# A new order for the compute queues of a linear-attention and gated-MLP kernel, and an earlier release of its weight loads

## The chip, the cores and the metric

The program runs on one core of one Trainium2 chip. The metric is the time of one execution on the device in microseconds (us). The kernel before took 202.53 us in the median of three runs (202.29 to 202.89). One execution was also taken with the hardware profiler; all rows of the profile in this document belong to that one execution.

The engines are named as the profile names them: PE (matmuls), PEld (its weight loads), DVE (vector engine), ACT (scalar engine), POOL (GpSimd) and SP (the queue that issues most DMAs).

## The reference

A block with 2048 rows of width 448: layer norm, an attention whose feature map is a pair of softmaxes, a projection and a residual; then layer norm, a gated MLP with 1792 hidden units, and a residual.

```python
def _A_ref(x, wqkv, w_phi, wo):            # B, S, D = 1, 2048, 448; H, Dh = 16, 28
    qkv = (x @ wqkv).reshape(B, S, 3, H, Dh).transpose(2, 0, 3, 1, 4)
    q, k, v = qkv[0], qkv[1], qkv[2]
    pq = jnp.einsum("bhsd,hdf->bhsf", q, w_phi)
    pk = jnp.einsum("bhsd,hdf->bhsf", k, w_phi)
    phi_q = jnp.concatenate([_softmax(pq), _softmax(-pq)], axis=-1)
    phi_k = jnp.concatenate([_softmax(pk), _softmax(-pk)], axis=-1)
    kv = jnp.einsum("bhsf,bhsd->bhfd", phi_k, v)
    z  = jnp.einsum("bhsf->bhf", phi_k)
    num = jnp.einsum("bhqf,bhfd->bhqd", phi_q, kv)
    den = jnp.einsum("bhqf,bhf->bhq", phi_q, z)[..., None] + 1e-6
    return (num / den).transpose(0, 2, 1, 3).reshape(B, S, D) @ wo

def _B_ref(x, w_gate, w_up, w_down):
    return (_sigmoid(x @ w_gate) * (x @ w_up)) @ w_down

h = x + _A_ref(_layernorm(x), A_wqkv, A_w_phi, A_wo)
h2 = h + _B_ref(_layernorm(h), B_w_gate, B_w_up, B_w_down)
```

## The kernel before

The 2048 rows are cut into 16 tiles of 128 rows. The text uses the names that the code gives to its operations; a trailing number is the tile, or the hidden unit's block of 128 after an underscore.

*First stage (to about 44 us), keys and values.* For each tile `x` is loaded, its statistics are taken on DVE (`bst`, `agg`, L545 and L546), the inverse deviation on POOL (`pow1`, L554) with a negated mean (`nm1`), and it is normalized (`xn`, L573 on DVE, L576 on POOL) into one of three buffers. It is transposed: the first four tiles by PE (`xT0` to `xT3`, L538) with a copy back by DVE or ACT (`xT0e` and so on, L531), the others by DMA from the SP queue. PE multiplies each tile by the folded key weight and by the value weight (`ppa`, `ppb` and `vva`, `vvb` for the first four tiles, then `pva`, `pvb`). Each such product is a pair: its "a" half fills the two row halves of the PE array with two PSUM banks, its "b" half fills them the other way around, so "b" waits until "a" has finished unless other PE work lies between. ACT takes two exponentials of the keys (`ek`, L671 and L672) and copies the values (`v1`, L531). DVE sums (`ss`, L675) and inverts (`rs`, L681), and DVE or POOL makes the normalized features (`phi`, L685) in one of three buffers. PE then adds the features times the values of a tile into two banks that live through the whole stage (`kva`, `kvb`). The query products (`pqa`, `pqb`) and their exponentials on ACT (`eq`, L721) lie between.

*Second stage (about 44 to 59 us), attention.* The finished sums are masked (`kvzA` to `kvzD`), PE forms the sums of the query features (`qs`) and the numerators (`num`), DVE turns these into quotients (`rsm`, `qq`, `b`, `c`, `rden`, L798 to L806), DVE or POOL writes the result (`o`, L810), which is transposed (`oT`) and multiplied by the output weight (`woa`, `wob`). The second normalization follows (`bs2`, `ag2`, `pow2`, `hn`, for later tiles `h`, `sq`, `ve`, `nm`), and a transposition (`hT`).

*Third stage (from about 59 us), the MLP.* PE computes gate and up products for two or four tiles at a time (`ga`, `gb`), ACT takes a tanh (`sig`, L925), DVE multiplies (`hh`, L926) and frees the PSUM banks; then PE does the down products (`dn`, `dp`, at the end `dm`), DVE adds the residual (`fin`, L961) and SP stores. Up to about 105 us the numerators of the remaining tiles and their output projections are interleaved.

*What sets the order.* Every engine executes its operations in the order that a table, `ORDER`, writes out by name, one string for each engine. Which of two engines executes an operation is also read from it: the operation runs on the engine whose string holds its name. Waits follow from the data: an operation waits for what it reads and for the readers of the buffer that it overwrites (`Graph.needs_wait`, `Graph.emit`). Between two operations on DVE, ACT or POOL a wait is added where the second reads the first's result. Two names on PE, `wwo` and `wgu`, do no work: they only wait for the loads of the output weight and of the gate and up weights, so that the first operation behind them takes these waits. `PACE` adds one more dependence: the load `ld_wg1` on the SP queue, and so all loads queued behind it (the rest of the gate, up and down weights), is held until a named PE operation is done.

Of the kernel before, what the change touches and what calls it, by code (L numbers as in the profile page):

```python
# [18 lines left out]
class Graph:  # L19
# [90 lines left out]
    def emit(self, nc):  # L110
# [153 lines left out]
    ),  # L264
    "dve": (
# [21 lines left out]
    ),  # L287
}
PACE = {"ld_wg1": "kva14"}
PROGRAM = (  # L290
# [35 lines left out]
def build(nc, A_x, A_wqkv, A_w_phi, A_wo, B_w_gate, B_w_up, B_w_down, out):  # L326
# [10 lines left out]
    with ExitStack() as es:  # L337
# [658 lines left out]
        at = {o.name: o.i for o in g.ops}  # L996
        for a, b in PACE.items():
            g.ops[at[a]].deps[at[b]] = False
# [36 lines left out]
```

## Time and profile before

| | us |
|---|---|
| median of three runs | 202.53 (202.29 to 202.89) |
| the profiled execution, whole | 202.7 |
| the profiled execution, span from its first to its last instruction | 200.8 |
| PE busy in the span | 195.5 |
| DVE busy in the span | 132.0 |
| ACT busy in the span | 89.4 |
| POOL busy in the span | 56.2 |
| granted TensorE clock, mean | 1.000 |

The span begins with the first instruction and ends with the last; 1.9 us of the execution lie around it. "Busy" counts overlapping instructions of an engine once. Matmuls are pipelined and their ends are modelled, so that a PE shown busy can still be held up for a tenth of a microsecond; the starts of its instructions tell more. Two views are used most below: the chain of waits, which goes back from the last instruction and says at each step what released it, and the timeline, which lists instructions of one engine in order of their start.

### The profile page before, as it was taken

Reading aid. Unit: us, or ns where it says so; the run is one execution under the profiler, and the core shown is the slowest. Engines: PE = TensorE matmul, PEld = TensorE weight load, DVE = VectorE, ACT = ScalarE, POOL = GpSimd, SP = SyncE. Lnnn points to the kernel's source line nnn. Section 1 sums busy time; section 2 is a strip of 40 time slices with the busy share of each in tenths; the row PEclk is TensorE's granted clock in tenths of the full one; section 3 lists DMA queues with packets and bytes.
Section 4 is the critical chain, followed back from the end, with each engine's and each line's share of the span. In section 5 each row is a group of like instructions: output and inputs, shape, how many; then the busy total and the mean of one; then the engine's idle time right before and its main releaser. Section 6 shows DMA issues by size and latency. Waiting matters only on the chain.

```text
span 200.8 us, 5854 instructions
## 1 busy us (share of the span) xinstructions
PE 195.5 (97%) x2516; PEld 114.4 (57%) x2516; DVE 132.0 (66%) x308; ACT 89.4 (45%) x174; POOL 56.2 (28%) x95
## 2 busy tenths in 40 slices
PE   7999999999999999999999999999999999999995
PEld 4835556565568778787444444555555555554443
DVE  5999999978888986576569877346332422272224
ACT  2668988898883451434232432324323212222220
POOL 5779948633343207510170110001400000000000
PEclk9999999999999999999999999999999999999999
DMA  6965346749984230360015220020312000004002
GB/s 157 316 140 129 54 83 76 221 144 302 309 206 66 52 57 15 66 82 3 0 29 124 56 42 10 20 58 26 65 38 52 0 3 2 0 3 137 0 3 91
DMA packets 32490, 16.26 MB, mean 81 GB/s; under 512 B 24720, under 2 KB 31568, under 8 KB 32464
## 3 DMA queue, kind: packets, MB, share of 16 engines
q1 hardware_dynamic: 32336, 15.86, 33.7%
q8 instruction: 20, 0.33, 0.7%
q14 instruction: 6, 0.05, 0.1%
q10 hardware_dynamic: 128, 0.03, 0.1%
HBM read 8.34 MB, written 1.84 MB: 51 GB/s over the span
## 4 chain that ended last, share of the span: by engine, by line
PE 92%; ACT 3%; DMA 2%; issue 1%; SPq 1%; DVE 0%
PE psum L309 84%; PE psum L954 5%; DMA wk_sb<-in_A_wqkv_dram 2%; ACT hhT L671 1%; ACT eq L721 1%; ACT hhT L672 1%; PE psum L524 1%; PE psum L538 1%; PE psum L612 1%; SPq L413 1%; PE psum L599 0%; ACT xnT L531 0%; ACT v L531 0%; DVE x_sb L961 0%
## 5 line engine op out<-in xcount | busy, mean ns | idle before, releaser
L309 PE MATMUL psum<-xnT,wu_sb 64*128 64x512 bf16 (+1 forms) x490 | 93.6, 333 | 0.0
L309 PE MATMUL psum<-xnT,wg_sb 64*128 64x512 bf16 (+1 forms) x490 | 93.5, 333 | 0.1
L925 ACT ACTIVATE sg_sb<-psum 128x512 bf16<-128x512 f32 x56 | 33.2, 596 | 90.1 <-PE psum L309 89.5
L926 DVE SCALAR_TENSOR_TENSOR hhT<-sg_sb,psum 128x512 bf16<-128x512 bf16 x56 | 37.7, 684 | 52.1 <-ACT sg_sb L925 51.7
L309 PEld LDWEIGHTS psum<-xnT,wg_sb 64*128 64x128 bf16 x490 | 44.6, 94 | 20.9 <-DVE hhT L926 2.5
L309 PEld LDWEIGHTS psum<-xnT,wu_sb 64*128 64x128 bf16 x490 | 44.7, 94 | 13.9
L309 PE MATMUL psum<-wd_sb,hhT 64*128 64x448 bf16 x336 | 37.3, 349 | 0.0
L309 PEld LDWEIGHTS psum<-wd_sb,hhT 64*128 64x128 bf16 x336 | 17.8, 94 | 14.2 <-DVE x_sb L836 0.5
L309 PE MATMUL psum<-Wk,xnT 64*128 64x448 bf16 x112 | 22.2, 350 | 0.5 <-ACT hhT L672 0.2
L309 PE MATMUL psum<-wv_sb,xnT 64*128 64x448 bf16 x112 | 22.3, 351 | 0.1
L810 POOL TENSOR_TENSOR o_pad<-c_sb,rden 128x448 bf16<-128x448 bf16 x11 | 10.2, 935 | 28.5 <-DVE rden L806 28.4
L675 DVE TENSOR_REDUCE ss<-hhT 128x32 f32<-128x896 bf16 x16 | 16.8, 1060 | 0.2 <-ACT hhT L672 0.2
L721 ACT ACTIVATE eq<-psum 120x1024 bf16<-120x1024 f32 x16 | 15.6, 1030 | 0.6 <-PE psum L309 0.4
L685 POOL TENSOR_TENSOR phi<-hhT,rs 128x896 bf16<-128x896 bf16 x8 | 13.6, 1710 | 5.6 <-DVE rs L681 3.4
L309 PE MATMUL psum<-xnT,Wq 64*120 64x512 bf16 x112 | 14.8, 383 | 0.3 <-ACT eq L721 0.2
L845 POOL TENSOR_SCALAR ve<-ssq 128x1 f32<-128x1 f32 x11 | 2.2, 201 | 41.8 <-ACT junk L842 41.5
L309 PE MATMUL psum<-wo_o,oT 64*128 64x448 bf16 x56 | 13.2, 350 | 0.0
L309 PE MATMUL psum<-wo_e,oT 64*128 64x448 bf16 x56 | 13.2, 349 | 0.0
L961 DVE SCALAR_TENSOR_TENSOR x_sb<-psum,x_sb 128x448 bf16<-128x448 f32 (+2 forms) x17 | 9.4, 592 | 2.9 <-PE psum L954 1.6
L954 PE MATMUL psum<-wd_sb,hhT 128*128 128x448 bf16 (+2 forms) x70 | 11.2, 316 | 0.0
L309 PEld LDWEIGHTS psum<-Wk,xnT 64*128 64x128 bf16 x112 | 7.8, 94 | 5.8 <-PE psum L309 1.0
L671 ACT ACTIVATE hhT<-psum 128x448 bf16<-128x448 f32 x16 | 8.8, 553 | 4.4 <-PE psum L309 4.2
(105 smaller groups left out, 234.4 us busy)
## 6 DMA issues: line engine op xcount, KB each, us to landing
out_dram<-x_sb SPq DMA_DIRECT2D x15, 112.0 KB, 1.8
x_sb<-in_A_x_dram SPq DMA_DIRECT2D x7, 224.0 KB, 4.2
wd_sb<-in_B_w_down_dram SPq DMA_DIRECT2D x7, 224.0 KB, 5.1
wg_sb<-in_B_w_gate_dram SPq DMA_DIRECT2D x3, 448.0 KB, 5.8
wu_sb<-in_B_w_up_dram SPq DMA_DIRECT2D x3, 448.0 KB, 5.7
wv_sb<-in_A_wqkv_dram SPq DMA_DIRECT2D x2, 224.0 KB, 4.7
wk_sb<-in_A_wqkv_dram SPq DMA_DIRECT2D x2, 196.0 KB, 4.1
wo_e<-in_A_wo_dram SPq DMA_DIRECT2D x1, 336.0 KB, 3.3
```

Of the source, the lines that this page charges most:

```text
L309: p = e.matmul(o, lhsT=w, rhs=r, start=st, stop=sp, tile_position=(row, 0))
L413: return op(eng, name, lambda e: e.dma_start(dst, src), r=r, w=w, dma="in" if eng == "sp" else "ain", nring=48 if eng == "sp" else 8, kb=kb)
L671: e.activation(ek[:, s, :, 0, :], src, ACT.Exp)
L675: op("dve", "ss%d" % t, lambda e: e.tensor_reduce(ss[:, s, :].rearrange("p (b h) -> p b h", h=2), eks.rearrange("p b (d h) -> p b h d", h= ...
L685: return e.tensor_tensor(phi[:, sp, :, :, :].rearrange("p b a n -> p (b a) n")[:, :, 0:56].rearrange("p b (d h) -> p b d h", h=2), eks.rea ...
L721: op("act", "eq%d_%d%s" % (c, i, "pm"[sg]), lambda e, sg=sg: e.activation(eq[c][:, sg, 2 * i:2 * i + 2, :].rearrange("p g n -> p (g n)"), ...
L810: return e.tensor_tensor(o_pad[:, t % NO, off:off + D].rearrange("p (h d) -> p h d", h=H), c_sb[:, t % NS, :, 0:DH], rden[:, t % NS, :][:, ...
L845: op(("pool", "dve"), "ve%d" % t, lambda e: e.tensor_scalar(ve2[:, t:t + 1], ssq2[:, t:t + 1], 1.0 / D ** 3, EPS, op0=ALU.mult, op1=ALU.ad ...
L925: op("act", "sig" + nm, lambda e: e.activation(sg_sb[:, k, 0:W], bk(bg)[:, 0:W], ACT.Tanh, scale=0.5), r=[B(bg)], w=[("sg", k)])
L926: op("dve", "hh" + nm, lambda e: e.scalar_tensor_tensor(out=dst, in0=sg_sb[:, k, 0:W].rearrange("p (f n) -> p f n", n=N), scalar=1.0, in1= ...
L954: p = e.matmul(bk(b)[:, lo:hi], lhsT=hb[:, ff, TS(t)], rhs=wd_sb[:, ff, lo:hi], start=ff == 0, stop=ff == FT - 1)
L961: op("dve", "fin%d%s" % (t, nm), lambda e: e.scalar_tensor_tensor(out=h_sb[:, t, lo:hi], in0=bk(b)[:, lo:hi], scalar=0.5, in1=h_sb[:, t, l ...
```

## The change

Two tables are changed and nothing else: no operation is added or taken away, every operation computes what it did, and the SP queue keeps its order.

`PACE` releases the load `ld_wg1` after `kva12` in place of `kva14`.

In `ORDER` the strings of ACT, PE, DVE and POOL are written anew. Some operations move to another engine: `v1_13` and `oT1e` from DVE to ACT; `kvzD` from DVE to ACT and `kvzA` the other way; `phi10` and `o1` from POOL to DVE and `phi5` from DVE to POOL; `nm1_8` from ACT to POOL; and, from the second normalization, `ve2`, `ve7`, `nm5`, `hn6`, `hn7` and `o10` from POOL to DVE and `ve3`, `ve6`, `nm2`, `nm3` from DVE to POOL. `wwo` moves from between `kva14` and `kvb14` to behind `dn0_11`, behind the first output product `woa0`; `wgu` moves forward to behind `gb0_5`.

```diff
     "act": (
-        "wphi wTe0 wTe2 wTe3 w2e0_0 w2e0_1 w2e0_2 par ek0 xT3e ek1 v1_0 v1_1 nm1_6 ek2 ek3 v1_2 w2e1_1 v1_3 nm1_8 "
...
+        "wphi wTe0 wTe2 wTe3 w2e0_0 w2e0_1 w2e0_2 par xT3e ek0 ek1 v1_0 v1_1 nm1_6 ek3 ek2 v1_2 w2e1_0 v1_3 w2e1_1 "
...
-PACE = {"ld_wg1": "kva14"}
+PACE = {"ld_wg1": "kva12"}
```

Three places show how instructions move. The first is ACT at about 11 us, at the head of the first stage. `COPY xnT` is the copy of tile 3's transpose, `xT3e`; each pair of rows L671 and L672 is one `ek`, for tiles 0 and 1.

```order
 L531 CAST Wk<-psum 128x8x2x28 x3
 L455 CAST par<-mask 128x2
+L531 COPY xnT<-psum 128x4x128
 L671 ACTIVATE hhT<-psum 128x8x56
 L672 ACTIVATE hhT<-psum 128x8x56
-L531 COPY xnT<-psum 128x4x128
 L671 ACTIVATE hhT<-psum 128x8x56
 L672 ACTIVATE hhT<-psum 128x8x56
```

The copy stood between the two `ek` and now stands ahead of both. On PE the transpose `xT3` that feeds it moves in the same way, from behind `ppb0` to between `ppa0` and `ppb0`.

The second place is POOL at about 23 to 28 us. Its rows L685 are `phi4`, the added `phi5`, and `phi7`; L554 is `pow1_12`, and the rows L576 are `xn13` and `xn15`.

```order
 L685 TENSOR_TENSOR phi<-hhT,rs 128x16x56
 L554 TENSOR_TENSOR rst<-mv,neghalf 128x4
+L685 TENSOR_TENSOR phi<-hhT,rs 128x16x56
 L576 TENSOR_SCALAR xn_pad<-x_sb,nm,rst 128x512
 L685 TENSOR_TENSOR phi<-hhT,rs 128x16x56
 L576 TENSOR_SCALAR xn_pad<-x_sb,nm,rst 128x512
```

`phi5` has come to POOL, directly behind `pow1_12`. On DVE, at the same time, these rows stand in the kernel after: `ss5`, `phi3`, `xn11`, `rs5`, `xn12`, `ss6` with `ss7`, `rs6`.

```order
L675 TENSOR_REDUCE ss<-hhT 128x32
L685 TENSOR_TENSOR phi<-hhT,rs 128x16x56
L573 TENSOR_SCALAR xn_pad<-x_sb,mv,rst 128x512
L681 RECIPROCAL rs<-ss 128x32
L573 TENSOR_SCALAR xn_pad<-x_sb,mv,rst 128x512
L675 TENSOR_REDUCE ss<-hhT 128x32 x2
L681 RECIPROCAL rs<-ss 128x32
```

`xn12` (the second row L573) stood behind `ss6` before and now stands right behind `rs5`. `xn12` reads what `pow1_12` writes, and `phi5` stands behind `pow1_12` on POOL, so both come free at nearly the same moment.

The third place is DVE in the MLP stage at about 74 to 78 us. Before, from `rsm9` to `o8`:

```order
L798 RECIPROCAL rsm<-psum 128x16
L799 TENSOR_TENSOR qq<-rsm,psum 128x16
L845 TENSOR_SCALAR ve<-ssq 128x1
L926 SCALAR_TENSOR_TENSOR hhT<-sg_sb,psum 128x2x256
L801 TENSOR_TENSOR b_sb<-psum,qq 128x464
L804 TENSOR_TENSOR c_sb<-b_sb,psum 128x464
L810 TENSOR_TENSOR o_pad<-c_sb,rden 128x448
```

And in the kernel after, again from `rsm9` to `o8`:

```order
L798 RECIPROCAL rsm<-psum 128x16
L799 TENSOR_TENSOR qq<-rsm,psum 128x16
L845 TENSOR_SCALAR ve<-ssq 128x1
L926 SCALAR_TENSOR_TENSOR hhT<-sg_sb,psum 128x2x256
L806 RECIPROCAL rden<-c_sb 128x16
L845 TENSOR_SCALAR ve<-ssq 128x1
L840 TENSOR_SCALAR nm<-sum 128x1
L801 TENSOR_TENSOR b_sb<-psum,qq 128x464
L804 TENSOR_TENSOR c_sb<-b_sb,psum 128x464
L840 TENSOR_SCALAR nm<-sum 128x1
L926 SCALAR_TENSOR_TENSOR hhT<-sg_sb,psum 128x2x256
L810 TENSOR_TENSOR o_pad<-c_sb,rden 128x448
```

The row L926 of the piece before is `hh0_12`; the two of the piece after are `hh0_10` and `hh0_12`. `hh0_12` stood ahead of `b9` and `c9` (L801, L804) and now stands behind them.

82 rows, old and new, of the table ORDER are left out of this document.

## The prediction

> **What bounds the kernel now.** I read the head of the page first, then DVE's forty slices of 5 us and the busy times by stage, then the chain of waits.
>
> ```profile
> span 200.8 us, 5854 instructions
> PE 195.5 (97%) x2516; PEld 114.4 (57%) x2516; DVE 132.0 (66%) x308; ACT 89.4 (45%) x174; POOL 56.2 (28%) x95
> DVE  5999999978888986576569877346332422272224
> PE 92%; ACT 3%; DMA 2%; issue 1%; SPq 1%; DVE 0%
> ```
>
> PE is busy for 195.5 of 200.8 us and holds 92% of the chain of waits. No PE work is removed, so the change can win only what PE waits. The stages show where another engine is full as well (start and end of the stretch, its length, then busy time of PE, PEld, DVE, ACT and POOL, clock, DMA share, GB/s):
>
> ```profile
> 18.00:44.00 26.00, 25.82 (x458) 15.60 (x458) 24.99 (x48) 23.16 (x51) 17.72 (x15) 1.00 0.52 116
> 44.00:59.00 15.00, 14.44 (x255) 8.41 (x249) 12.65 (x37) 13.27 (x19) 5.74 (x7) 1.00 0.97 256
> ```
>
> From 18 to 44 us DVE is busy for 24.99 of 26.00 us: what PE gains at the start counts only if DVE keeps up to tile 15. The places where the chain leaves PE (start, length, what):
>
> ```profile
> 11.34 0.54 ACT hhT L671
> 11.88 0.43 ACT hhT L672
> 12.32 0.48 ACT xnT L531
> 12.79 0.45 ACT hhT L671
> 13.24 0.45 ACT hhT L672
> 13.69 0.14 issue
> 13.82 0.95 PE psum L309 x8
> ...
> 17.45 0.43 ACT v L531
> ...
> 18.02 2.49 PE psum L309 x30
> ...
> 43.55 0.14 issue
> 43.69 0.43 PE psum L309 x16
> 44.12 0.05 issue
> ...
> 47.20 1.95 ACT eq L721 x2
> ...
> 49.19 1.07 PE psum L309 x8
> ```
>
> `ppa2` at 13.82 waits for ACT's `ek0`, `xT3e`, `ek1`; `pva4` at 18.02 waits for the next link of the same ACT queue; `pqa2_1` at 49.19 waits for two `eq`.
>
> **The start.** `xT3e` now runs before `ek0`, while ACT is idle waiting for `ppb0`. Its 0.48 us leave the chain, and `ek1` ends at about 13.2. PE must then be ready earlier too. It is: `xT3` now fills the wait between the halves of `ppa0`/`ppb0`, and `seed` that of `vva0`/`vvb0`. `xT2` slips about 0.2 on DVE behind `agg4`, `agg5`, yet `vva0` starts about 0.1 earlier; `vvb0` ends its issue near 13.37, so `ppa2` starts there: 0.45 earlier. `ppb2`, `ek2`, `v1_2` and `pva4` follow by the same 0.45. Lower bound 0, if `xT2` slips further; upper bound the 0.48 of the row. I take **-0.45**.
>
> **The middle of the first stage.** A lone `kva` between two halves leaves a hole:
>
> ```profile
> 42.22 0.39 PE L309 MATMUL psum<-v,phi 64*128 64x58 bf16 x16
> 42.45 0.86 PE L309 MATMUL psum<-xnT,Wq 64*120 64x512 bf16 x6
> ```
>
> Two kv products issue in 42.45 - 42.22 = 0.23, one in 0.115. `kvb2` moved into the hole behind `pva8` saves **-0.1**; `kvb7` saves nothing, since `pva13` waits there for ACT's `v1_11` anyway. The waits of `wwo` stood between `kva14` and `kvb14`: 0.14 of issue there against 0.05 between `kva15` and `kvb15`, **-0.08**; `woa0` takes them over while it waits for `oT1e`, so they cost nothing there, and 0.1 if that cover is gone. Together -0.63 by `kvb15`.
>
> Can DVE follow? Its last products and the work it hands over:
>
> ```profile
> 42.22 1.14 DVE L685 TENSOR_TENSOR phi<-hhT,rs 128x896 bf16<-128x896 bf16 x2
> L685 DVE TENSOR_TENSOR phi<-hhT,rs 128x896 bf16<-128x896 bf16 x8 | 4.6, 591 | 0.0
> L531 DVE CAST v<-psum 128x448 bf16<-128x448 f32 x1 | 0.6, 617 | 0.0
> ```
>
> It loses `phi5` (0.59) and `v1_13` (0.62) and gains `phi10` (0.59), net 0.6 less, but `xn14` comes early enough to wait about 0.3 for POOL's `xn13`. I put `phi15`'s end at 42.9 against 43.36 now; `kva15` (now 0.115 behind the kv product at 43.69, so 43.8) may then start about 0.14 after that, at 43.05, and PE wants it at 43.2. The 0.14 is the step from the chain above, 13.69 to 13.82. So DVE just keeps up. If it kept its present 43.36, `kva15` could start at 43.5 and 0.3 of the gain would stay. I cap the sum at **-0.55**.
>
> **The loads** leave two kv products earlier, about 2 us. They start now at 43.6 and have all landed before the MLP needs them at 59; no transposition is in flight at 41. Zero, from 0 to -0.1 (`oT2` would find a shorter DMA backlog, but the output product that needs it is not waiting).
>
> **The second stage.** `pqb1_1` moves ahead of `num1`: its `eq` starts 0.23 earlier (two kv-size products issue in that time) and `pqa2_1` with it. It is given back, for `o1` is now DVE work:
>
> ```profile
> 48.47 1.83 POOL L810 TENSOR_TENSOR o_pad<-c_sb,rden 128x448 bf16<-128x448 bf16 x2 [6.24 <-DVE rden L806]
> 49.11 0.17 DVE L799 TENSOR_TENSOR qq<-rsm,psum 128x16 f32<-128x16 f32 x1
> 49.31 0.64 DVE L801 TENSOR_TENSOR b_sb<-psum,qq 128x464 bf16<-128x464 f32 x1
> 58.44 0.42 DVE L531 COPY xnT<-psum 128x512 bf16<-128x512 bf16 x1
> L810 DVE TENSOR_TENSOR o_pad<-c_sb,rden 128x448 bf16<-128x448 bf16 x5 | 3.1, 625 | 0.1
> ```
>
> `o1` goes in at about 49.4 and moves `b2`, and so `c2`, by 0.64. Queued behind on DVE are `rsm3` to `rden3` and the statistics of the second norm; who waits is `num3`, then `hn0`, `hT0`. Taking `oT1e` to ACT returns 0.42 of it, but `rden4` now stands ahead of `hT0e`, so the copy at 58.44 that releases the MLP comes about **0.16 later** on the shifted clock. Bounds: -0.23 (the `eq` gain stays) to +0.3.
>
> **The MLP stage.** `hh0_12` frees the banks for `ga2_0`, which now stands ahead of `gb2_2`:
>
> ```profile
> 75.88 0.26 DVE L798 RECIPROCAL rsm<-psum 128x16 f32<-128x16 f32 x1 [0.70 <-PE psum L309]
> 76.33 0.68 DVE L926 SCALAR_TENSOR_TENSOR hhT<-sg_sb,psum 128x512 bf16<-128x512 bf16 x1
> 76.92 0.63 DVE L801 TENSOR_TENSOR b_sb<-psum,qq 128x464 bf16<-128x464 f32 x1
> 77.59 0.64 DVE L804 TENSOR_TENSOR c_sb<-b_sb,psum 128x464 bf16<-128x464 bf16 x1
> ```
>
> `rsm9` runs near 73.7 instead of 75.88, since `num9` is earlier; then come `hh0_10`, `b9`, `c9` and `hh0_12` at about 76.5 to 77.2, and `ga2_0`, which PE would reach at 77.1 where it is at 77.76 now, starts at 77.33. This wait contains the 0.16: both come down the same DVE queue, so PE loses **+0.23** in all by then. Bounds 0 to +0.4.
>
> **Sum.** -0.55 + 0.23 = -0.32 on the profiled execution, which is 202.70 whole (span 200.8 and 1.9 around it): 202.38. The median of the runs is 0.17 below that execution, so I predict **202.2**.
>
> **Rival 1, a lock between DVE and POOL (slower).** What an overlap of the two costs is in these rows:
>
> ```profile
> 25.64 1.01 POOL L554 TENSOR_TENSOR rst<-mv,neghalf 128x4 f32<-128x4 f32 x1 [0.23 <-DVE mv L546]
> 27.13 0.77 POOL L576 TENSOR_SCALAR xn_pad<-x_sb,nm,rst 128x512 bf16<-128x512 bf16 x1 [0.49 <-ACT hhT L672]
> 25.70 0.32 DVE L573 TENSOR_SCALAR xn_pad<-x_sb,mv,rst 128x512 bf16<-128x512 bf16 x1
> 27.18 0.87 DVE L573 TENSOR_SCALAR xn_pad<-x_sb,mv,rst 128x512 bf16<-128x512 bf16 x1 [0.16 <-issue]
> 23.55 1.87 POOL L685 TENSOR_TENSOR phi<-hhT,rs 128x896 bf16<-128x896 bf16 x1 [0.28 <-DVE rs L681]
> 30.98 1.69 POOL L685 TENSOR_TENSOR phi<-hhT,rs 128x896 bf16<-128x896 bf16 x1 [3.08 <-DVE rs L681]
> ```
>
> `xn12`, begun 0.05 after POOL's `xn13`, took 0.87 where `xn11` took 0.32, and ended just after `xn13` did. In the new order POOL's neighbour is `phi5`, not an `xn`, and a `phi` takes 1.69 on POOL. `pow1_12` ends at 26.65 now, behind three losses on POOL: 0.28 that `phi4` waits for `rs4`, 0.18 that it lost beside DVE's `phi3` (1.87 against 1.69) and 0.23 for `agg15`. `rs4` and `agg15` come earlier in DVE's new order and `phi3` later, so `pow1_12` ends about 0.7 earlier, near 25.9. `xn12` can then start at 26.0, and `phi5` at 26.1, when `kvb2` has freed its buffer: `xn12` is first by 0.1, less than the 0.2 to which I can place either. If `phi5` is first, `xn12` ends at 28.2, `ss6`, `ss7` and `xn14` follow it, `phi15` ends near 44.2 and `kvb15` runs about 0.53 later than now instead of 0.55 earlier. With the 0.23 that is +0.76: **203.3**. It decides from the moment that POOL passes `pow1_12` before DVE passes `rs5` and `kvb2` is done. For it: the margin; against it: an early `kvb2` is the only thing that lets `phi5` go at all.
>
> The Trainium skill, in "SBUF — State Buffer", section "Who interferes with whom", says that a vector `tensor_scalar` that uses both ports and any GpSimd instruction exclude each other, and that whichever issues first holds the shared ports for its whole length. The rows of `xn12` and `xn13` agree (0.87 against 0.32), and by that rule the loser here is blocked for the whole of `phi5`, which is this rival and not the forecast.
>
> **Rival 2, nothing is given back (faster).** If DVE's queue has more room in both later stages than I count, the -0.63 stays and 0.1 more at `pqa2_1`: **201.8**. For it: from 75 us on DVE's slices fall to 6 and 5 tenths. Against it: from 60 to 75 us, where this chain runs, they read 8, 9 and 8.
>
> **Rival 3, the change does not do what it says:** the earlier loads and the `wwo` move change nothing that PE waits for, and DVE stays at its 43.36: gain 0.3 less 0.23, **202.5**. It lies within the forecast's own range.
>
> **Chances.** Forecast with rival 3: 0.42, own range 201.8 to 202.7. Rival 1: 0.33. Rival 2: 0.25. About 0.3% (0.6 us) is what a measurement of this kernel tells from no change. Faster by more than that (below 201.92): nearly all of rival 2 and a fifth of the forecast, 0.24 + 0.08 = 0.32. Slower (above 203.14): nine tenths of rival 1, 0.30. Within: 0.38. The range 201.5 to 203.4 takes in rival 1 and rival 2 with their bounds.
>
> **What would show it.** In the profile after: `ppa2` near 13.4 and `pva4` near 17.6; `xn12` 0.3 to 0.4 long just after 26.0, or 1.7 to 2 long with `phi5` beside it; `phi15` ending near 42.9; DVE's copy `hT0e` near 58.1; an idle of 0.1 to 0.3 of PE before `ga2_0` near 76.8; and nothing on PE that ends on a load. The forecast is wrong if `pva4` does not come earlier, if `xn12` loses, or if PE waits after 80 us where it does not now.

## The result and the profile after

The changed kernel took 204.0 us in the median of six runs (203.74 to 204.64), the kernel before 202.5 us: a ratio of 1.0077 with a 95% interval of 1.006 to 1.0094. It is 1.5 us slower, where 0.3 faster was forecast, and it lies above the range (201.5 to 203.4). The profiled execution took 203.94 us, with a span of 201.8. That is 1.24 more than the profiled execution before; 1.0 of it is span and 0.2 lies around the span, and nothing in the traces explains those 0.2.

First the head of the page after, with DVE's slices and the engines' shares of the chain of waits:

```profile
span 201.8 us, 5849 instructions
PE 195.9 (97%) x2516; PEld 112.7 (56%) x2516; DVE 134.4 (67%) x309; ACT 90.8 (45%) x175; POOL 53.5 (26%) x93
DVE  5899999988898996775678977436432422272224
PE 83%; POOL 6%; DVE 4%; DMA 4%; issue 1%; SPq 1%; DVEq 0%
```

PE's work is what it was, but its share of the chain fell from 92% to 83%. POOL (6%) and DVE (4%) have come in, and the share of DMA has doubled from 2% to 4%. The busy times of the stretch from 18 to 44 us (its length, then PE, PEld, DVE, ACT and POOL) say where:

```profile
18.00:44.00 26.00, 24.97 (x424) 14.45 (x422) 25.44 (x46) 22.25 (x48) 18.23 (x15) 1.00 0.51 121
```

PE is busy for 0.85 less than before in the same 26 us (24.97 against 25.82), and DVE is full (25.44). The chain of waits in this stretch (start, length, what) went through PE alone (but for one issue of 0.14) from 18 to 44 us before. Now it reads:

```profile
17.15 0.75 POOL xn_pad L576
17.91 0.20 POOL nm L553
18.11 0.30 POOL rst L554
18.41 4.05 DMA xnT<-xn_pad
22.47 0.09 issue
22.56 0.36 POOL xn_pad L576
...
23.31 0.77 POOL xn_pad L576
24.08 1.65 POOL phi L685
25.74 1.36 POOL rst L554
...
27.20 1.69 DVE xn_pad L573
28.89 1.99 DVE ss L675 x2
...
31.71 1.94 POOL phi L685
...
34.50 1.70 POOL phi L685
```

From top to bottom: `xn7` on POOL, the transposition of tile 7 by DMA (4.05 us, landing at 22.47), `xn10` and `xn9`, which wait for it because `xn10` overwrites the buffer that tile 7 is read from, then `phi4`, `pow1_12`, and on DVE `xn12`, `ss6`, `ss7`. At its end stands `phi8`, for which PE's `kva8` waits at 36.25. The timeline of POOL and DVE shows what they lose beside each other (start, length, and in brackets the idle time before and its releaser):

```profile
22.56 1.52 POOL L576 TENSOR_SCALAR xn_pad<-x_sb,nm,rst 128x512 bf16<-128x512 bf16 x2 [0.84 <-DMA xnT<-xn_pad]
24.05 1.69 POOL L685 TENSOR_TENSOR phi<-hhT,rs 128x896 bf16<-128x896 bf16 x1
24.80 1.42 DVE L685 TENSOR_TENSOR phi<-hhT,rs 128x896 bf16<-128x896 bf16 x1
25.70 1.39 POOL L554 TENSOR_TENSOR rst<-mv,neghalf 128x4 f32<-128x4 f32 x1
27.06 1.68 POOL L685 TENSOR_TENSOR phi<-hhT,rs 128x896 bf16<-128x896 bf16 x1
27.20 1.69 DVE L573 TENSOR_SCALAR xn_pad<-x_sb,mv,rst 128x512 bf16<-128x512 bf16 x1 [0.39 <-POOL rst L554]
```

The first row holds `xn10` and `xn9`, 0.84 late for want of tile 7. DVE's `phi3` lies beside POOL's `phi4` and takes 1.42 in place of about 0.6. `pow1_12` lies beside `phi3` and ends at 27.08. `phi5` starts at 27.06, `xn12` at 27.20, and `xn12` stays until `phi5` is done: 1.69 where 0.4 is its usual length. With the 0.39 of idle ahead of it DVE loses 2.5 us in this place (0.8 with `phi3`, 0.4 idle, 1.3 with `xn12`), against 0.6 before (0.16 idle and about 0.45 with `xn12`), and `phi15` ends at 44.80 in place of 43.36. PE starts `kvb15` at 45.23 in place of 44.17, 1.06 later. That is rival 1's mechanism, later and dearer than it was priced.

The start came as forecast, and the later stages did not:

```profile
13.36 1.74 PE L309 MATMUL psum<-Wk,xnT 64*128 64x448 bf16 x14
17.56 0.35 PE L309 MATMUL psum<-Wk,xnT 64*128 64x448 bf16 x1 [0.18 <-ACT v L531]
```

`ppa2` starts at 13.36 and `pva4` at 17.56 (13.4 and 17.6 were forecast). PE is 1.06 late at `kvb15`, 1.03 at `woa2`, 1.04 at `ga8_1` near 124 us: the later stages give nothing back and take nothing.

### The profile page after: what moved, and what is told of

It is laid out like the page before. It is cut to its first block, busy times and chain, and to the rows that moved or that the text cites. A ratio compares the mean times of both kernels' runs of the same rounds, so it can differ in the third digit from the quotient of the medians.

```text
span 201.8 us, 5849 instructions
## 1 busy us (share of the span) xinstructions
PE 195.9 (97%) x2516; PEld 112.7 (56%) x2516; DVE 134.4 (67%) x309; ACT 90.8 (45%) x175; POOL 53.5 (26%) x93
## 4 chain that ended last, share of the span: by engine, by line
PE 83%; POOL 6%; DVE 4%; DMA 4%; issue 1%; SPq 1%; DVEq 0%
PE psum L309 75%; PE psum L954 5%; POOL phi L685 3%; DMA wk_sb<-in_A_wqkv_dram 2%; DMA xnT<-xn_pad 2%; POOL xn_pad L576 2%; DVE ss L675 1%; PE psum L538 1%; DVE xn_pad L573 1%; POOL rst L554 1%; PE psum L524 1%; SPq L413 1%; DVE st L545 1%; PE psum L612 0%; DVE rs L681 0%
## 5 line engine op out<-in xcount | busy, mean ns | idle before, releaser
L926 DVE SCALAR_TENSOR_TENSOR hhT<-sg_sb,psum 128x512 bf16<-128x512 bf16 x56 | 37.8, 685 | 52.3 <-ACT sg_sb L925 51.9
L810 POOL TENSOR_TENSOR o_pad<-c_sb,rden 128x448 bf16<-128x448 bf16 x9 | 8.4, 937 | 32.6 <-DVE rden L806 32.6
L685 POOL TENSOR_TENSOR phi<-hhT,rs 128x896 bf16<-128x896 bf16 x8 | 13.7, 1720 | 5.9 <-PE psum L309 3.7
L845 POOL TENSOR_SCALAR ve<-ssq 128x1 f32<-128x1 f32 x11 | 2.2, 202 | 45.2 <-ACT junk L842 44.9
L801 DVE TENSOR_TENSOR b_sb<-psum,qq 128x464 bf16<-128x464 f32 x16 | 10.1, 630 | 0.7 <-PE psum L309 0.6
```

The source lines that it names most:

```text
L685: return e.tensor_tensor(phi[:, sp, :, :, :].rearrange("p b a n -> p (b a) n")[:, :, 0:56].rearrange("p b (d h) -> p b d h", h=2), eks.rea ...
L801: op("dve", "b%d" % t, lambda e: e.tensor_tensor(h3(b_sb), OMv[:, :, :, 0:EV], h2(qq)[:, :, :, None].to_broadcast([P, NB, 8, EV]), ALU.mul ...
L810: return e.tensor_tensor(o_pad[:, t % NO, off:off + D].rearrange("p (h d) -> p h d", h=H), c_sb[:, t % NS, :, 0:DH], rden[:, t % NS, :][:, ...
L845: op(("pool", "dve"), "ve%d" % t, lambda e: e.tensor_scalar(ve2[:, t:t + 1], ssq2[:, t:t + 1], 1.0 / D ** 3, EPS, op0=ALU.mult, op1=ALU.ad ...
L926: op("dve", "hh" + nm, lambda e: e.scalar_tensor_tensor(out=dst, in0=sg_sb[:, k, 0:W].rearrange("p (f n) -> p f n", n=N), scalar=1.0, in1= ...
```

## The experiments

Two theories were put against each other. **A**: the order of DVE and POOL behind `pow1_12` (`phi5` on POOL, `xn12` ahead of `ss6`) makes the loss. **B**: tile 7's late landing makes it, and the lock only passes it on. All times are medians; the kernel before took 202.45, 202.62, 202.55, 202.44 and 202.47 us beside the five groups of runs, in this order.

**One operation of the change moved: a_xn12, a_phi5, a_phi0, and the start alone: b_start**

```diff
 a_xn12, DVE:   -rs5 xn12 ss6 ss7         +rs5 ss6 xn12 ss7
 a_phi5:        -POOL pow1_12 phi5 xn13   +POOL pow1_12 xn13, DVE xn12 phi5 ss6
 a_phi0, POOL:  -phi0 xn6 xn7             +xn6 phi0 xn7
 b_start (against the kernel before):
   ACT:  -par ek0 xT3e ek1       +par xT3e ek0 ek1
   PE:   -ppa0 ppb0 warm9 xT2 xT3 vva0 vvb0     +ppa0 xT3 ppb0 warm9 xT2 vva0 seed vvb0
   POOL: -nm1_3 pow1_2 xn3       +nm1_3 xn3 pow1_2
```

> The changed kernel with one operation moved: on DVE xn12 goes back behind ss6, so that ss6 runs while POOL holds the ports for phi5. Theory A (the loss is DVE's queue in the first stage, and what xn12 loses beside phi5 is lost to everything behind it): ss6 runs from 26.8 to 27.9 inside the time that xn12 spent blocked, xn12 still ends near 28.9 when phi5 ends, and ss7 and all behind it come about 1.0 us earlier (ss7 ends near 29.9 in place of 30.88, phi15 near 43.8 in place of 44.80): 203.1 us against 204.0. Theory B (the loss is the late transposition of tile 7, which holds up xn10, phi4 and pow1_12 on POOL; the lock only follows from it): pow1_12 ends at 27.1 as it does now, and less than half of the loss goes: 203.6 to 204.0.

> The changed kernel with phi5 back on DVE, right behind xn12, and xn13 next on POOL. Theory A (lock): xn12 starts at 27.2 as now but shares its time only with xn13 (0.77), so it ends near 28.0 in place of 28.89; phi5 then costs DVE 0.6, and everything behind is 0.3 earlier: 203.7 us. If it were POOL's own load that is late (phi7, phi8 and phi9 come behind phi5 there) and not DVE, POOL would be free 1.68 earlier and the time would fall to 203.0 or less. Theory B (tile 7's late transposition): 203.9 to 204.0.

> The changed kernel with xn6 back ahead of phi0 on POOL, so that the transpositions of tiles 6 and 7 are issued earlier, as before. Theory B (the late transposition of tile 7 is the root): tile 7 lands near 21.0 in place of 22.47, xn10 starts near 21.8, pow1_12 ends near 26.0, xn12 is first, and nearly the whole loss goes: 202.2 to 202.6 us. Theory A (the order behind pow1_12 is the cause whenever it comes): pow1_12 ends 0.5 earlier, phi5 again starts within 0.05 of its end and before xn12, xn12 again takes 1.6 or more, and only those 0.5 are won: 203.5.

> The kernel before with the edits of the start alone: xT3e ahead of ek0 on ACT, xT3 behind ppa0 and seed behind vva0 on PE, xn3 ahead of pow1_2 on POOL. If the forecast's first term is right and DVE has room: ppa2 near 13.4, pva4 near 17.6, and 202.1 us against 202.5. If DVE bounds PE up to tile 15 (phi15 ends at 43.36 and kva15 follows it): the first 0.45 is won up to about 40 us and part of it lost again by kvb15: 202.2 to 202.4. No gain (202.5) if PE only waits elsewhere.

`a_xn12` 203.39 us (ratio to before 1.0055, 1.0036 to 1.0073), `a_phi5` 203.54 (1.0047, 1.003 to 1.0063), `a_phi0` 204.06 (1.007, 1.0054 to 1.0087), `b_start` 202.47 (1.0002, 0.9979 to 1.0024). DVE's `xn12` in `a_xn12` and then in `a_phi5` (whose table is one line longer, so that its lines count one more):

```profile
27.98 1.22 DVE L573 TENSOR_SCALAR xn_pad<-x_sb,mv,rst 128x512 bf16<-128x512 bf16 x1
```

```profile
27.12 0.41 DVE L574 TENSOR_SCALAR xn_pad<-x_sb,mv,rst 128x512 bf16<-128x512 bf16 x1 [0.39 <-POOL rst L555]
```

0.9 and 1.1 of the 1.5 stay, so either move is worth 0.4 to 0.6 us, less than half of the loss. `a_xn12` lies between what A (203.1) and B (203.6 to 204.0) had given it, `a_phi5` nearer to A (203.7) than to B. `a_phi0` looked like a miss for B, but its trace shows that it did not try B: tile 7 was issued at 18.40 and landed at 22.59, as late as in the change. `b_start` brought `pva4` 0.37 forward as measured from `ppa0`, the first product of the stage, and its trace keeps that to the end; but its runs spread from 201.82 to 204.75 and their median shows no gain.

**POOL without the wait for tile 7, the later stages alone, the loads alone, and a version of parts: a_xn9, b_later, a_pace, best1**

```diff
 a_xn9, POOL:  -phi2 xn10 xn9 phi4   +phi2 xn9 xn10 phi4
 b_later: before up to kvb15, phi15, phi13 and eq1_0p, then the change
 a_pace:  -PACE = {"ld_wg1": "kva12"}   +PACE = {"ld_wg1": "kva14"}
 best1:   b_later with b_start's edits, PACE kva14,
   ACT: ek13 +v1_13 eq0_0m      DVE: ss12 -v1_13 rs11
```

> The changed kernel with xn9 ahead of xn10 on POOL, so that POOL does not wait for the landing of tile 7 (the buffer that xn10 overwrites) but goes on at once with the buffer of tile 6, which lands 2.9 us earlier. Nothing moves on DVE. Theory B (POOL is late because of tile 7, and that is the root): xn9 starts at 21.8, phi4 near 23.4 in place of 24.05, pow1_12 near 25.0 in place of 25.70, phi3 on DVE loses only 0.2 to phi4 in place of 0.82, and most of the loss goes: 202.4 to 202.8 us. Theory A (DVE loses its time at two places, beside phi4 and beside phi5, and only the first depends on POOL being late): about 0.6 to 0.9 of DVE's loss goes, xn12 still stands blocked for 1.5 or more beside phi5: 203.2 to 203.5. No effect (204.0) if neither holds.

> The order before up to the end of the first stage (kvb15 on PE, phi15 on DVE, phi13 on POOL, eq1_0p on ACT), then the new order for all that is left, with wwo and PACE as the change has them. The forecast's term (o1 on DVE, rden4 ahead of hT0e, hh0_12 behind b9 and c9 cost 0.23 in all): 202.7 us against 202.45 before. What the trace after the change suggests (the shift of PE is 1.06 at kvb15 and 1.04 at the end of the span, so the later stages give nothing back): 202.4, with ga2_0 not held up. A gain of 0.3 or more (202.15) would mean that the later stages of the change are worth having by themselves.

> The changed kernel with the weight loads paused until kva14, as before. If the loads cost nothing either way: 204.0 us, the same as the change. If the earlier loads hurt (their packets stand ahead of PE's instruction fetch near 44 us, or they slow the transpositions): 203.6 or less. If the later loads make PE or a transposition wait (the last down weights land after 60 us): more than 204.2.

> A version of parts: the order before for the middle of the first stage on DVE and POOL, the start of the change (xT3e ahead of ek0, xT3 and seed between the halves, xn3 ahead of pow1_2), v1_13 on ACT, which takes 0.62 from DVE, the new order for the later stages, wwo as the change has it, and the loads paused as before. If DVE's time in the first stage is what counts, it keeps up with the earlier start: 202.0 to 202.1 us against 202.45. If the start's gain is lost to something else than DVE (ACT, which gets v1_13, or a transposition): 202.4.

`a_xn9` 203.31 us (1.0035, 1.0021 to 1.0049): 0.7 won. POOL hardly waited for tile 7 there (`phi4` at 23.46, 23.55 in the kernel before), but `xn12` again took 1.69 beside `phi5`, and 0.7 of the loss stayed, as A had said (203.2 to 203.5). `b_later` 202.53 (1.0004, 0.9993 to 1.0015): the later stages are worth nothing either way, and the forecast's +0.23 is not there. `best1` 202.56 (1.0005, 0.9981 to 1.0028), with runs from 201.94 to 204.25. `a_pace` 204.49 (1.0095, 1.0077 to 1.0112): with the loads at `kva14` the change loses about 0.4 more, which the intervals, as they overlap, do not part from nothing, but the trace has a place for it. Its chain of waits at `woa2`:

```profile
55.97 3.67 DMA oT<-o_pad
59.63 0.14 issue
59.77 4.39 PE psum L309 x81
```

The transposition of tile 3's attention output lands at 59.63 and PE waits for it; in the change it lands at 58.30 and `woa2` runs at 59.17.

**Both places mended, the version of parts with earlier loads, and two single parts of the change in the kernel before: a_both, best2, b_pace, b_phi5**

```diff
 a_both:  a_xn9 and a_phi5 together
 best2:   best1 with PACE kva12
 b_pace:  -PACE = {"ld_wg1": "kva14"}   +PACE = {"ld_wg1": "kva12"}
 b_phi5:  -DVE ss7 phi5 phi6, POOL pow1_12 xn13   +DVE ss7 phi6, POOL pow1_12 phi5 xn13
```

> The changed kernel with xn9 ahead of xn10 on POOL and phi5 back on DVE behind xn12: both places at which DVE loses its time are mended. Theory A (DVE's lost time in the first stage is the whole loss, and its parts add): 0.7 from the one and 0.5 from the other, 202.8 us, and PE's shift at kvb15 against the profile before falls from +1.06 to about -0.2 to +0.1. If the two share one cause, it is no better than the better of them: 203.3.

> The version of parts (start of the change, v1_13 on ACT, the order before for the rest of the first stage, the new order for the later stages), now with the loads paused until kva12 as the change has them. In the version with kva14 tile 3's attention output landed at 57.77 and held woa2 up by 0.22. If the loads are what ate the start's gain: 202.2 to 202.3 us against 202.5 before. If it is lost elsewhere: 202.5.

> The kernel before with only the weight loads paused until kva12 in place of kva14. The forecast's term: nothing waits for the loads there (woa2 starts 0.9 after tile 3's attention output has landed), so 202.5 us as before. If earlier loads delay PE's instruction fetch near 43 us or the last transpositions of the first stage: 202.8 or more.

> The kernel before with only phi5 moved to POOL, behind pow1_12 and ahead of xn13. There xn12 stands behind ss6 on DVE, so that ss6 runs while POOL holds phi5. xn12 then ends about 0.4 later (near 28.5 in place of 28.05) and DVE is rid of phi5's 0.6: 202.4 to 202.5 us, no loss. If phi5 on POOL is by itself what costs the time (the shared ports, or xn13 and tile 13 coming 1.2 later): 203.0 or more.

`a_both` 203.15 us (1.0037, 1.0024 to 1.0049): between 202.8, if the parts add, and 203.3, if they share one cause. Its trace does not decide it, for tile 7 landed at 23.20 there and held `phi4` up to 24.02. `b_phi5` 202.74 (1.0007, 0.9996 to 1.0017): `phi5` on POOL is no loss by itself, although `xn12` took 1.27 in its trace. `best2` 202.59 (1.0034, 1.0006 to 1.0062) fell into two groups, seven runs from 202.07 to 202.60 and five from 203.52 to 204.90. So did `b_pace` (202.29; 0.9997, 0.9981 to 1.0013): eight from 202.17 to 202.49, three from 203.27 to 203.50. The profiled execution of `b_pace` is of the upper group, and PE stands still in it, in the middle of a product (PE's timeline):

```profile
46.53 1.48 PE L309 MATMUL psum<-xnT,Wq 64*120 64x512 bf16 x11
48.44 0.64 PE L309 MATMUL psum<-xnT,Wq 64*120 64x512 bf16 x3 [0.42 <-issue]
```

"issue" means that PE waited for nothing that the profile shows. The fetch of a block of PE's instructions, which the DMA records show at 43.18 in the trace before, begins at 45.89 here, after the weight loads have begun, and PE goes on 1.5 us after its end. In the profiled execution of `a_xn12`, 204.96 us and also far above the median of its kernel, the fetch begins at 47.28 and PE stands for 1.33 (its chain of waits):

```profile
48.59 1.33 issue
49.91 2.20 PE psum L309 x29
```

**Tile 7 early or late against the order: h_early, h_mid, h_early12, and the loads once more: b_pace2**

```diff
 h_early: the change, with DVE and POOL as before up to ss2 and phi2:
   POOL: -xn3 pow1_2 nm1_4 pow1_4 xn4 xn5 pow1_6 phi0 xn6 xn7 nm1_8 pow1_8 xn8 phi2
         +xn3 pow1_2 pow1_4 nm1_4 xn4 pow1_6 xn5 xn6 phi0 xn7 pow1_8 xn8 phi2
   DVE:  -bst7 bst4 bst5 agg4 agg5 xn2 bst8 xT2e bst6 ss0 agg7 agg8 agg6 rs0 ... ss2
         +bst7 bst5 bst4 xn2 agg5 agg4 agg7 bst6 xT2e agg6 ss0 bst8 rs0 bst9 ... ss2
   ACT:  -ek3 ek2 v1_2 w2e1_0 v1_3 w2e1_1   +ek2 ek3 v1_2 w2e1_1 v1_3 nm1_8 w2e1_0
   PE:   -xT2 warm9 ... w2m1_1 w2m1_0   +warm9 xT2 ... w2m1_0 w2m1_1
 h_mid:   the change up to ss2, phi2, v1_4 and pvb5, then before to the end of the
          first stage, then the change
 h_early12: h_early with a_xn12's move
 b_pace2: b_pace again
```

> The changed kernel, but DVE and POOL in the order before up to ss2 and phi2 (near 20 us; the start on PE and ACT is the change's but for what stands beside nm1_8 and ek2), so that tile 7 is transposed early. Theory B (tile 7's late landing, 22.47, is the root): tile 7 lands near 20.6, phi4 starts near 23.5, pow1_12 ends near 26.4, and the time is 202.5 us or less. Theory A (the order behind pow1_12): xn12 again loses 1.3 beside phi5 and 203.2 to 203.5 us stay, since only what POOL's lateness cost is won.

> The changed kernel up to ss2 on DVE, phi2 on POOL, v1_4 on ACT and pvb5 on PE, then the order before to the end of the first stage, then the change again. Tile 7 stays late. Theory A (the order of DVE and POOL from 20 to 30 us is the cause): 202.3 to 202.6 us, DVE loses less than 1 us to waits and to POOL. Theory B (tile 7): POOL's xn10 still waits to 22.5, and 203.2 us or more stay.

> h_early with xn12 behind ss6 as well. If both causes count and add (0.6 to 0.7 each): 202.6 us. If they overlap: as h_early.

> The kernel before with the loads paused until kva12, a second time. Theory of the fetch: in two thirds to four fifths of the executions PE's instruction block that it needs near 48 us is fetched before 44 us and the time is 202.2 to 202.5; in the others the fetch starts behind the weight loads, 2 to 3 us later, PE stands still for 0.6 to 1.4 near 48 us, and the time is 203.2 or more. If the slow ones have another cause, a slow execution's trace shows no such stop of PE.

`h_early` 202.28 us (0.9992, 0.9977 to 1.0008), nine of twelve runs from 202.00 to 202.44, three from 202.94 to 205.11 (its trace is of 202.94): the loss is gone, with the order behind `pow1_12` unchanged. `h_mid` 204.24 (1.0088, 1.0064 to 1.0113): with the order of before behind a late tile 7 the loss stays whole. Its trace has a short stop of PE near 49 us (0.40) as well, but `kvb15` is late ahead of it already (45.56, 1.39 later than before), and two transpositions are late: POOL's `xn10` waits for tile 7 as in the change, and DVE's `xn14` waits 1.48 for tile 11 (landing at 31.89); what each of the two costs cannot be told apart. So A, the order alone, falls. B does not hold in full either: `a_xn9` took most of tile 7's delay off POOL and kept 0.7 of the loss, and `h_early` moves DVE's operations up to `ss2` together with tile 7, so it does not show which of the two did it. `h_early12` 202.81 (1.0013, 0.9989 to 1.0038) had six runs from 201.96 to 202.58 and six from 203.03 to 204.43; its trace is of the upper group and has tile 7 landing at 22.58. `b_pace2` 202.74 (1.0009, 0.9995 to 1.0023) showed no upper group in eleven runs, so the share of such executions is not settled.

POOL and then DVE of `h_early`, at the place where the change lost 1.69:

```profile
23.46 1.69 POOL L685 TENSOR_TENSOR phi<-hhT,rs 128x896 bf16<-128x896 bf16 x1 [0.17 <-DVE rs L681]
25.11 1.11 POOL L554 TENSOR_TENSOR rst<-mv,neghalf 128x4 f32<-128x4 f32 x1
26.52 1.77 POOL L685 TENSOR_TENSOR phi<-hhT,rs 128x896 bf16<-128x896 bf16 x1 [0.30 <-DVE rs L681]
```

```profile
25.24 0.61 DVE L685 TENSOR_TENSOR phi<-hhT,rs 128x896 bf16<-128x896 bf16 x1
26.09 0.35 DVE L681 RECIPROCAL rs<-ss 128x32 bf16<-128x32 f32 x1
26.36 0.39 DVE L573 TENSOR_SCALAR xn_pad<-x_sb,mv,rst 128x512 bf16<-128x512 bf16 x1
```

`xn12` reads what `pow1_12` wrote, and `phi5` reads `rs5`. Here `pow1_12` ends 0.22 before `rs5`: POOL has to wait for DVE, `xn12` follows `rs5` on its own queue, and it loses nothing. In the change `pow1_12` ends 0.28 after `rs5`: DVE waits, and `phi5` follows at once. The engine that comes last wins the port. In the first case it costs POOL 0.3, in the second DVE 1.7. Which case it is goes with `phi3` on DVE: in the nine traces with this order of DVE (up to `rs5`) in which `phi3` begins before `phi4` ends on POOL, `pow1_12` takes 1.39 to 1.46 and ends 0.28 after `rs5`; in the two, `h_early` and `h_fetch`, in which it begins 0.09 after `phi4`'s end, `pow1_12` takes 1.11 and ends 0.22 before `rs5`.

**The fetch moved: a_fetch, h_fetch**

What delays tile 7? The DMA records of all traces hold fetches of instructions (20 of them in the page after, "q8 instruction"), which are taken to be PE's because a shorter queue on PE moves them, as the last two runs will show. One begins near 20.4 us, about when tile 7's transposition ends:

| kernel of the trace | tile 7 issued, us | fetch begins after the issue, us | tile 7 landed after the issue, us |
|---|---|---|---|
| before, b_later, b_phi5, best2 | 18.08 to 18.27 | 2.47 to 2.70 | 2.46 to 2.48 |
| b_pace, b_pace2, h_early | 18.24 to 18.33 | 2.30 to 2.38 | 2.46 to 2.48 |
| best1, b_start | 18.02, 18.33 | 2.21, 2.18 | 2.47, 2.49 |
| a_phi0, a_pace | 18.40, 18.45 | 2.16, 2.12 | 4.19, 4.13 |
| h_early12, a_xn9, a_xn12 | 18.14 to 18.53 | 2.04 to 2.06 | 4.25 to 4.50 |
| the change, h_mid, a_phi5 | 18.40 to 18.43 | 1.94 to 1.98 | 4.00 to 4.14 |
| a_both | 18.61 | 2.40 | 4.59 |

But for `a_both`, a fetch that begins 2.18 us or more after the issue does tile 7 no harm (tile 8 then lands 3.15 to 3.68 us after its own issue, against 2.45 to 3.34 in the other rows), and one that begins within 2.16 us costs the transposition 1.5 to 2.0 us. A landing is told by sixteen updates of a semaphore. In the change fifteen of tile 7's come by 20.96, in time, and only the last at 22.47, 1.18 after the end of the fetch. In all nine late landings of the table, `a_both` among them, the last update comes 1.05 to 1.28 after the fetch's end. The last two runs move the fetch and leave the transposition where it is:

```diff
- ... (6, 128), (4, 128), (6, 128), (8, 128), (2, 128)):
+ ... (6, 128), (4, 128), (6, 128), (1, 128), (2, 128)):
```

> The changed kernel with one of the fill-in products that keep PE's clock up (warm8, near 9 us) cut from 8 matmuls to 1; they compute nothing that is read. PE's block of instructions that was fetched from 20.39 is then fetched about 0.8 later, when tile 7 has landed. Theory (the fetch holds up tile 7's transposition, and this lateness is the whole loss): tile 7 lands 2.5 us after its issue, near 20.9 in place of 22.47, POOL's xn10 starts near 21.8, xn12 on DVE does not lose to phi5, and the time is 202.1 to 202.6 us in place of 204.0. If the order of DVE and POOL is the cause, or another transfer delays tile 7: 203.8 to 204.2.

> h_early with the same cut of warm8. h_early ran at 202.0 to 202.4 us in nine executions and at 202.9 to 205.1 in three; its tile 7 escaped the fetch by 0.02 us in the trace. Theory: with the fetch 0.8 later no execution is hit by it, all lie within 0.5 us, and the median is 202.1 us, faster than both kernels. If the slow ones have another cause (PE's later fetch among the weight loads near 45 us), they stay, at the same share.

`a_fetch` 204.2 us (1.0075, 1.0049 to 1.0101), `h_fetch` 203.33 (1.0042, 1.0029 to 1.0054). The part on tile 7 came out: the fetch begins at 22.27 and 21.76, and tile 7 lands 2.57 and 2.46 us after its issue. In `a_fetch` that issue was at 18.59, later than in the change. The delay went with the fetch: tile 8, which landed 2.8 us after its issue in the change and 3.6 in `h_early`, now takes 4.1 and 4.5. The part on the time failed, for two reasons that the traces name. The first is in POOL and then DVE of `a_fetch`:

```profile
23.36 1.69 POOL L685 TENSOR_TENSOR phi<-hhT,rs 128x896 bf16<-128x896 bf16 x1
25.00 1.46 POOL L554 TENSOR_TENSOR rst<-mv,neghalf 128x4 f32<-128x4 f32 x1
```

```profile
24.97 0.63 DVE L685 TENSOR_TENSOR phi<-hhT,rs 128x896 bf16<-128x896 bf16 x1
```

POOL was not late: `phi4` ended at 25.04, in `h_early` at 25.15. But `phi3` had begun 0.07 ahead of that end, so `pow1_12` took 1.46 and ended 0.28 after `rs5` once more, `xn12` took 1.69 again, and tile 12's transposition, which it starts, met the next fetch (at 29.67). The second: the later fetch, now at 47.11 and 46.25, left PE without instructions in both profiled executions. From the chain of waits of `a_fetch`:

```profile
28.30 4.68 DMA xnT<-xn_pad
32.98 0.05 issue
33.02 1.74 PE psum L309 x30
...
48.59 1.05 issue
49.63 0.56 PE psum L309 x11
```

`h_fetch` stands for 1.05 too, at 47.70. If all its runs had this stop, it would stand at 202.3 without, an estimate; its `kvb15` starts at 43.72, 0.45 earlier than before (0.37 of it because `ppa0` began earlier in that execution) and 1.5 earlier than in the change. Three of the eight runs of `a_fetch` lie from 203.14 to 203.20, as if without the stop, five from 204.08 to 205.03.

No version was shown to beat the kernel before; `h_early` comes nearest (202.28 against 202.44, an interval that holds 1).

## Why the prediction was wrong, point by point

**The start, -0.45: right, slightly too large.** `pva4` came 0.46 earlier, but `ppa0` itself started 0.09 earlier in that execution; it lies anywhere from 9.18 to 9.81 us in the twenty traces. Measured from `ppa0`, the edits' own share is 0.37, in the change and in `b_start`. It is no constant: `pva4` starts 8.46 after `ppa0` in all five traces without these edits and 8.08 to 8.42 in the fifteen with them, a share of 0.04 to 0.38. It did not show in the median of `b_start`. That the earlier PE also brings its fetch forward, to within 0.02 of where it does harm, speaks for collisions in some of those runs; only one execution of it has a trace, so this stays open.

**The middle, -0.1 and -0.08.** The hole behind `pva8` cannot be read in the change, since `kva3` waited there for `phi3`. `wwo`'s share was right: in `b_later`, which has it moved and nothing else on PE in the first stage, `kvb14` starts 0.11 earlier.

**"`pow1_12` ends about 0.7 earlier, near 25.9" is the step that failed.** It ended at 27.08. I worked it out from `rs4`, `agg15` and `phi3` on DVE, and left out what POOL's own queue waits for ahead of them: `xn10` needs the buffer of tile 7. In the change `phi0` stands ahead of `xn6`, so the transposition of tile 6 was issued 0.95 later (17.18 against 16.23), and the SP queue came to tile 7 only when that issue was done, 0.30 later (18.41 against 18.11; `xn7` itself ended 0.17 earlier). The earlier start also brought PE's fetch 0.21 forward (20.39 against 20.60). So they met, and tile 7 landed 1.89 later. The trace before had such a late landing already (tile 13, 3.9 us after its issue), and I gave it no term. The three losses of POOL, about 0.7, that I had seen leave did leave; in their place `xn10` began 0.81 later (22.56 against 21.75), and `pow1_12` itself took 1.39 in place of 1.01. `a_fetch` shows that the fetch decides the landing. That the landing decides the time is shown for about half of the loss: 0.7 stays in `a_xn9` and in the three lower runs of `a_fetch`, and in the traces of both kernels `phi4` is early and `pow1_12` still ends after `rs5`; nothing stays in `h_early`, where tile 7 is in time and `pow1_12` ends first. The other half goes with the next point.

**"`xn12` is first by 0.1": the condition was the wrong way around.** I wrote that the lock decides against DVE when POOL passes `pow1_12` before DVE passes `rs5`. I had overlooked that `phi5` reads `rs5`. It is the reverse: `xn12` took 1.69 in all five traces with this order in which `pow1_12` ended after `rs5` (each by 0.28), and 0.39 in the two in which it ended before (by 0.22). The chance of 0.33 was put on the right mechanism for the wrong reason.

**Rival 1's price, +0.76, was too low.** It had +0.53 at `kvb15` and 0.23 behind it; `kvb15` came 1.06 later and nothing was added behind it. Left out were `phi3` beside `phi4` (0.8 more for DVE, for which `kva3` waits: PE's lead falls from 0.51 to 0.09 there) and the 0.39 of idle ahead of `xn12`. `phi15` ended at 44.80, where this rival had 44.2. The page "SBUF — State Buffer" of the Trainium skill, section "Who interferes with whom", says that a DVE `tensor_scalar` that uses both ports and an instruction of GpSimd exclude each other for a whole instruction; the row of `xn12`, 1.69 long and ending 0.15 after `phi5`, agrees.

**The loads, 0: right in the kernel before, probably wrong in the change.** `b_pace2` has the time of before; in the change the earlier loads seem to be worth about 0.4 (`a_pace`), since `woa2` then no longer waits for tile 3's attention output. My zero rested on 0.9 us of slack (the landing at 57.24, `woa2` at 58.14). In `a_pace` that transposition is issued 1.64 later than in the kernel before, where PE is 1.17 later at `kvb15`, and lands 3.67 after its issue in place of 2.91: the slack is used up. Whether the upper group of times is the price of the earlier loads stays open: `b_pace` had it in three runs of eleven, `b_pace2` in none, and `best1` and `b_start`, with the loads at `kva14`, have single runs of 204.25 and 204.75.

**The later stages, +0.23: nothing.** The stall that I moved on ended in an idle that I had not looked for. DVE before, then DVE after:

```profile
53.81 1.17 DVE L829 BATCH_NORM_STATS2 st<-psum 128x6 f32<-128x448 f32 x2 [0.52 <-PE psum L309]
```

```profile
52.72 0.26 DVE L798 RECIPROCAL rsm<-psum 128x16 f32<-128x16 f32 x1 [0.54 <-PE psum L309]
54.85 1.17 DVE L829 BATCH_NORM_STATS2 st<-psum 128x6 f32<-128x448 f32 x2
```

The second norm's statistics waited 0.52 for PE's output product before. That wait is gone, because `rsm3` to `rden3` come 0.5 later against PE: `rsm3` now waits 0.54 for `num3`, which stands behind `pqb2_1` on PE in the new order (52.28 against 50.75). `o1` runs ahead of that wait, and nothing on PE waits for it. So `hT0e` kept its distance from PE (+1.12 at its start against +1.06 at `kvb15`), and `ga2_0` did not stall.

## What to carry to other kernels

- Before pricing a reordering, follow each engine's queue back to the buffers that it overwrites: here a POOL operation waited for the DMA of another tile, and that DMA landed 1.9 us later than before.
- Where two engines share a port and each needs the other's last result, the one that finishes first has to wait and loses; compare the two finishing times, not the starts. Here 0.07 us of another pair of operations (`phi3` and `phi4` in `a_fetch`) turned the two around.
- A tuned order has edges that no view shows: instruction fetches move with PE's position in its program, and a gain of 0.4 us at the start can push one into a transfer. Take the distances of the fetches to the landings of such transfers from the DMA records, and prefer an order with half a microsecond to spare.

## What was not expected of the hardware

- A DMA transposition can lose 1.5 to 2.0 us to a fetch of PE's instructions (16 KB, 0.9 to 1.6 us in these records). Tile 7 was late in all eight traces in which the fetch began up to 2.16 us after its issue, and in one of the twelve in which it began later; the late landings follow the fetch's end by 1.05 to 1.28 us, and the delay moved to tile 8 when the fetch was moved. The edge is not sharp: tile 12 and the next fetch, near 30 us, give late landings (3.5 to 4.7 us after the issue) in all 16 traces with 0.84 to 2.11 us between issue and fetch, but 2.42 in the kernel before, with 2.13, and 4.72 in `h_early`, with 2.36. The Trainium skill, "Runtime: NRT & Kernel Launch", section "Instruction fetch mechanics", calls the cost of a block's boundary mostly hidden. For PE that is so in most rows; for a transfer beside it it is not.
- PE can run out of instructions. In five of the twenty traces a fetch that begins at 43.1 to 45.2 in the others began at 45.9 to 47.3, and PE stood for 0.4 to 1.3 us near 48 to 50 and went on 1.4 to 1.6 us after that fetch's end. All five have the weight loads at `kva12`, as have ten of the other fifteen, and in `a_fetch` and `h_fetch` the cut had moved the fetches as well. That the loads hold the fetch up is suggested by this but was not tested by itself.
- The queue that is on the spot takes a shared port first: `phi5` started 0.02 before the end of `pow1_12`, `xn12`, released by the same instruction on another engine, 0.12 after it.
